# Half as many warming products from the second group on, and PSUM banks dealt anew between three kinds of tile

## The chip, the cores and the metric

The kernel runs on one core of a Trainium2 chip. The metric is device time in microseconds (us), from the start of the execution to its end, as the median of several runs. The core's engines are TensorE (PE, whose weight loads are listed apart as PEld), VectorE (DVE), ScalarE (ACT), GpSimd (POOL) and SyncE (SP), whose queue issues most of the transfers between DRAM and the on-chip memory. TensorE writes its products to PSUM, which has eight banks here: a tile of 128 x 512 numbers of four bytes fills one.

## The reference

Three layers follow each other, with 4 batches, 8 heads, 768 steps and a head size of 48.

```python
# layer 1: a delta-rule scan over t, per batch and head
k_n = k / (norm(k) + 1e-6)
y[t]  = q[t] @ state
state = state + beta[t] * outer(k_n[t], v[t] - k_n[t] @ state)
# layer 2: x = y with heads side by side
u, v = split(gelu(x @ w_in)); v = layernorm(v) * g_ln
x = x + (u * (w_sg @ v + b_sg)) @ w_out
# layer 3: xk, xr mix x with the step before it
out = sigmoid(xr @ w_r) * (relu(xk @ w_k)**2 @ w_v)
```

## The kernel before, in words

The scan is cut into 12 chunks of 64 steps. Two chunks make a *group*, so there are six groups, 0 to 5. The 32 pairs of batch and head are held in two halves, `o` = 0 and 1. A chunk of a half goes through six stages, each a burst of small products and then one step on another engine that the next stage needs:

- `st_rq` (L444, L446): keys times state into tile `rk`, and the query products into tile `qk`. Then DVE forms the residual `r` (L424), ACT copies `qk` out (L453) and POOL masks it (L454).
- `st_d0` (L432): the solver's matrix times `r`. Then ACT copies out `u` (L461).
- `st_l` (L468): a correction into `rk`. Then DVE forms `r` again (L424).
- `st_d1` (L432 again): the second solve. Then ACT copies the result to `SQ` (L479).
- `st_s` (L488): the new state into `sps`. Then ACT copies it out (L494).
- `st_y` (L502): the output `y` into a tile `ms`. Then ACT copies it to `yst` (L507) and SP sends it on as `xT` (L523, L527).

The two halves run three stages apart, so TensorE alternates between them: 24 *points* (places in the program at which one stage of one half stands) make a group. On PE, DVE, ACT and POOL the instructions stay in the order in which this code writes them. SP's order is made by the compiling layer.

At each point other work is put around the stage. `background` gives DVE (with ACT and POOL behind it) a slice of the next group's triangular solver (L321 to L412), of a layer norm (L586 to L602), and of a weight's conversion (`narrow`, L157 to L168). `fill` gives TensorE work of layer 2 for the previous group: `v` products (L567, then Gelu on ACT at L576) and `u` products (L618, Gelu at L622), and every other point of a stretch also the key products of a later group (`gram`, L298 and L300, copied out at L307). Where `fill` has no such work left it calls `keep_warm` (L659), which multiplies a zero tile `warm` by itself: a 128 x 128 weight load and a 128 x 512 product, into a tile `ms` that nobody reads. How many there are comes from the stage's entry in `UNITS`, in units of one such product, with the fraction carried over in `idle`. In a steady group the layer's work runs out for eight points in a row, around the group's start.

PSUM is dealt out so: `sps0` and `sps1` have a bank each, and the pool `ps2` gives two banks to `rk`, two to `qk` and two to `ms`. `ms` is what `bank()` returns, and `gram`, `st_y`, the `v` and `u` products and `keep_warm` all share it in turn. A tile that is asked for waits until the tile which held its bank before has been read out.

After the scan follow layers 2 and 3, in which all eight banks belong to one pool, and which the change doesn't touch.

Of the kernel before, what the change touches and what calls it, by code (L numbers as in the profile page):

```python
# [7 lines left out]
F32 = mybir.dt.float32  # L8
# [12 lines left out]
P = 128  # L21
C = 64
# [6 lines left out]
LJ = 2  # L29
LJ0 = 7  # L30
SV = 60
B0 = 1.4
PRE = 0.8
GRAM0 = 17
# [40 lines left out]
def fused_kernel(  # L75
# [144 lines left out]
    with ExitStack() as at:  # L220
# [3 lines left out]
        ps2 = at.enter_context(tc.tile_pool(name="ps2", bufs=2, space=PSUM))  # L224
# [34 lines left out]
        banks = [ps2]  # L259

        def bank():
            return banks[0].tile([P, 8, C], F32, name="ms")

        Sps = [ps1.tile([P, 8, D], F32, name=f"sps{o}") for o in range(2)]
        warm = ap1.tile([P, P], mybir.dt.bfloat16, name="warm")
# [17 lines left out]
        def gram(g, parts=((0, 64),)):  # L283

            GD = ap1.tile([P, 32, NU], F32, name="GD")
            GL = ap2.tile([P, NU, 32], F32, name="GL", bufs=NGL)
            GLs[g] = GL

            def half(i, c0, c1, j):
                t = kT[2 * g + i // 2]  # L290
                if j == 0:
                    GDs["ps"] = bank()
                gps = GDs["ps"]
                for p in range(4 * j, 4 * j + 4):
                    u = (i % 2) * 8 + p
                    for h in range(2):
                        r = 64 * (1 - h)
                        T.matmul(gps[r:r + 32, p, c0:c1], lhsT=t[r:r + 64, u, 0:32],  # L298
                                 rhs=t[r:r + 64, u, c0:c1], start=True, stop=True)
                        T.matmul(gps[r + 32:r + 64, p, c0:c1], lhsT=t[r:r + 64, u, 32:64],  # L300
                                 rhs=vw2(t, r, 64, u * C + 32, [(0, (c1 - c0) // 32), (1, 32)]),
                                 start=True, stop=True)
                if j:
                    for x, c in ((GD[:, :, 8 * i:8 * i + 8].rearrange("p j u -> p u j"), 0),
                                 (GL[:, 8 * i:8 * i + 8, :], 32)):
                        if c0 <= c < c1:
                            A.activation(x, gps[:, :, c:c + 32], AF.Copy, scale=-1.0)  # L307

            GDs[g] = GD
            return [[(-GU, lambda i=i, j=j, c=c: half(i, *c, j)) for j in range(2)]  # L310
                    for c in parts for i in range(4)]
# [104 lines left out]
        def scale_v(s):  # L416
            G.tensor_tensor(vt[s], vt[s], vw(neTs[s // 2], NPR * (s % 2), [(1, NPR), (0, D)]),
                            op=ALU.mult)
# [3 lines left out]
        def residual(s, o):  # L422
            t = ap2.tile([P, 8, D], F32, name="r32")
            V.tensor_tensor(t, vt[s][:, 8 * o:8 * o + 8, :], RQs[o][:, :, 0:D], op=ALU.add)  # L424
            RQs[o, "r"] = t
# [10 lines left out]
        def st_rq(s, o):  # L436
            cur, k0 = SQ[o][s % 2], 8 * o
            R = RQs[o] = ps2.tile([P, 8, D], F32, name="rk")
            Q = ps2.tile([P, 8, C], F32, name="qk")
            for p in range(8):  # L440
                for h in range(2):
                    r, b0 = 64 * (1 - h), 64 * h
                    k = kT[s][r:r + 64, k0 + p, :]
                    T.matmul(R[r:r + 64, p, :], lhsT=k, rhs=cur[h][r:r + 64, p, 0:D],  # L444
                             start=(p == 0), stop=True, skip_group_check=True)
                    T.matmul(Q[b0:b0 + 64, p, :], lhsT=k, rhs=cur[h][r:r + 64, p, D:],  # L446
                             start=(p == 0), stop=True, skip_group_check=True)
            yield
            residual(s, o)
            for h in range(2):  # L450
                b0 = 64 * h
                pt = cur[h][b0:b0 + 64, :, D:]
                A.activation(pt, Q[b0:b0 + 64], AF.Copy, scale=-1.0)  # L453
                G.affine_select(out=pt, in_=pt, pattern=[[0, 8], [1, C]],  # L454
                                compare_op=ALU.is_gt, fill=0.0, base=0, channel_multiplier=-1)
# [40 lines left out]
        def st_y(s, o):  # L496
            g, cur = s // 2, SQ[o][s % 2]
            yps = bank()
            for p in range(8):
                for h in range(2):  # L500
                    b0 = 64 * h
                    T.matmul(yps[b0:b0 + 64, p, :], lhsT=cur[h][:, p, 0:64],  # L502
                             rhs=cur[h][:, p, D:], start=True, stop=True)
            yield
            if s % 2 == 0:
                ysts[o] = ap2.tile([P, 8, P], F32, name="yst")
            A.activation(ysts[o][:, :, C * (s % 2):C * (s % 2) + C], yps, AF.Copy, scale=-1.0)  # L507
            if s + 2 < 12:
                load_q(s + 2, o)
            if s % 2:  # L510
                store_x(g, o, ysts[o])
                after(LAGX, lambda: x_split(g, o))
            if o == 1:
                if s + 2 < 12:
                    load_tok(s + 2)
                    after(4, lambda: scale_v(s + 2))
                load_k(s + NKT)
# [15 lines left out]
        later, vstat, streams, point = [], {}, [], [0, 0]  # L533

        def after(n, f):
            later.append((point[0] + n, f))
# [95 lines left out]
        def fill(n):  # L632
            n += owed[0]
            while n > 0 and (units or opened[0]):
                if not opened[0]:
                    done = min([i for i, _ in running] + [n_jobs - len(jobs)])
                    ready = [u for u in units if done >= (6, 12)[u[2]]]
                    if ready:
                        units.remove(ready[0])
                        opened[0] = ready[0][1]()  # L640
                    else:
                        break
                w, f = opened[0].pop(0)
                f()
                n -= w
            owed[0] = min(n, 0)
            if n > 0 and point[0] < 144:
                idle[0] += n
                keep_warm(int(idle[0]))
                idle[0] -= int(idle[0])  # L650

        idle = [0]

        def keep_warm(n):

            if n > 0:
                o = bank()[:].rearrange("p a b -> p (a b)")
                for _ in range(n):
                    T.matmul(o, lhsT=warm, rhs=vw(warm, 0, [(0, 4), (1, P)]), start=True, stop=True)  # L659

        def background(t):

            for e in [e for e in later if e[0] <= point[0]]:
                later.remove(e)
                e[1]()
            i = 0
            while t > 0:
                ready = [e for e in streams if e[0] <= point[0]]
                if not ready:
                    return  # L670
                kinds = [[e for e in ready if e[2] == k] for k in ("ln", "solve")]
                kinds.append([e for e in ready if any(e[1] is j for _, j in running[:2])])
                turn = [k[0] for k in [kinds[j] for j in TURN[point[1]]] if k]
                e = turn[i % len(turn)]
                try:
                    c = next(e[1])
                    if isinstance(c, tuple):
                        e[0] = point[0] + c[0]
                        if c[0] == 0:
                            c[1]()  # L680
                        elif c[1] is not None:
                            after(c[0], c[1])
                    else:
                        t -= c
                    i += 1
                    streams.remove(e)
                    streams.append(e)
                except StopIteration:
                    streams.remove(e)
                    running[:] = [r for r in running if r[1] is not e[1]]  # L690
# [31 lines left out]
        def whole(job):  # L722
            for _, f in job:
                f()

        stages = [st_rq, st_d0, st_l, st_d1, st_s, st_y]
        rest = [lambda j=j: whole(j) for j in diag[4:]]
        k = 0
        while any(e[2] == "solve" for e in streams):
# [9 lines left out]
            if 0 in neTs and 1 not in GDs:  # L739
                after(SV, lambda: scale_v(1))  # L740
                body = st_rq(0, 0)
# [14 lines left out]
        def run(fn, s, o):  # L756
# [11 lines left out]
            if point[0]:  # L768
                background(BUDGET[stages.index(fn)] * (B0 if g == 0 else 1))
            while len(jobs) > n_rest and len(running) < RUN[0]:  # L770
# [20 lines left out]
        while opened[0]:  # L791
            fill(1)
# [164 lines left out]
    ms = {}  # L957
# [112 lines left out]
```

## Time and profile before

| | us |
|---|---|
| time, median of 3 runs | 815.54 (814.7 to 817.19) |
| the profiled execution, its own time | 811.44 |
| its span, first to last instruction | 809.7 |
| PE busy in the span | 747.1 (92%) |
| DVE busy | 583.3 (72%) |
| ACT busy | 344.3 (43%) |
| POOL busy | 186.9 (23%) |
| mean granted TensorE clock | 0.970 |

The profile is of one execution, and its time lies 4.1 us under the median of the others. Times within it count from the span's start. The stage loop begins at about 50 us, its group 1 at 103, group 2 at 160.6, group 3 at 213.8, group 4 at 267 and group 5 at 314; the scan's last stage ends near 374. A matmul's end is modelled, and a new one starts before the one ahead has ended, so for PE the distances from start to start tell more than the busy share. A bracket behind a row of the timeline gives the idle time of that engine before it and what ended it.

### The profile page before, as it was taken

How to read it: one execution, taken by the hardware profiler on the slowest of the kernel's cores; microseconds unless marked ns; L12 is line 12 of the kernel's file. 1: busy time of each engine (PE TensorE's matmuls, PEld its weight loads, DVE VectorE, ACT ScalarE, POOL GpSimd, SP SyncE). 2: the span in 40 equal slices, each digit the busy share in tenths (PEclk: the TensorE clock that was granted, in tenths of full speed). 3: DMA queues.
4: the chain of work that ended last, by engine and by line, in shares of the span. 5: the costliest groups of instructions: out<-in, count | busy, mean ns of one | idle time of the engine just before them, and what ended most of it. 6: DMA issues, size and time to landing. Idle time of an engine off the chain costs nothing.

```text
span 809.7 us, 23901 instructions
## 1 busy us (share of the span) xinstructions
PE 747.1 (92%) x10206; PEld 656.5 (81%) x10206; DVE 583.3 (72%) x1253; ACT 344.3 (43%) x681; POOL 186.9 (23%) x197
## 2 busy tenths in 40 slices
PE   3368999999999998978989899899999999999998
PEld 3335667768778676767889799799999999999998
DVE  7989999689699698234779896988945655653442
ACT  2213454465555644634632231316744544542331
POOL 4125342232131323323324453340000000000000
PEclk9978999999999999989999889899999999999999
DMA  8403353354353443437987646449200000000000
GB/s 231 90 27 100 91 118 87 95 155 140 94 150 83 132 121 92 137 99 184 277 266 247 202 128 194 145 127 292 59 30 21 20 20 20 20 21 30 11 20 30
DMA packets 84970, 89.21 MB, mean 110 GB/s; under 512 B 25856, under 2 KB 68992, under 8 KB 84864
## 3 DMA queue, kind: packets, MB, share of 16 engines
q1 hardware_dynamic: 80128, 78.64, 32.8%
q0 software_dynamic: 4736, 9.04, 4.2%
q8 instruction: 80, 1.31, 0.7%
q14 instruction: 26, 0.21, 0.1%
HBM read 56.86 MB, written 26.08 MB: 102 GB/s over the span
## 4 chain that ended last, share of the span: by engine, by line
PE 60%; DVE 18%; DMA 7%; issue 6%; POOL 3%; ACT 2%; SPq 2%; DVEq 0%; POOLq 0%; ACTq 0%
PE ms L139 32%; PE ms L618 5%; PE ms L659 4%; PE rk L432 3%; PE ms L567 3%; PE ms L298 2%; DVE tmp L321 2%; PE ms L884 2%; DMA raw<-in_w_k_dram 2%; PE ms L502 2%; PE rk L468 2%; PE sps L488 2%; PE rk L444 2%; POOL na L168 1%; DVE na L157 1%
## 5 line engine op out<-in xcount | busy, mean ns | idle before, releaser
L168 POOL TENSOR_TENSOR na<-raw,na 128x256 f32<-128x256 f32 (+2 forms) x43 | 40.2, 938 | 149.7 <-DVE raw L167 110.0
L659 PE MATMUL ms<-warm 128*128 128x512 bf16 x222 | 62.1, 405 | 9.0 <-DVE warm L407 9.0
L139 PE MATMUL ms<-wvh,sh 128*128 128x384 f32 x192 | 64.9, 338 | 0.0
L139 PE MATMUL ms<-wvl,sh 128*128 128x384 f32 x192 | 64.9, 338 | 0.0
L139 PE MATMUL ms<-wvh,sl 128*128 128x384 f32 x192 | 64.8, 338 | 0.0
L139 PE MATMUL ms<-xm_hi,wkh 128*128 128x384 f32 x192 | 64.1, 334 | 0.0
L139 PE MATMUL ms<-xm_lo,wkh 128*128 128x384 f32 x192 | 64.1, 334 | 0.0
L139 PE MATMUL ms<-xm_hi,wkl 128*128 128x384 f32 x192 | 64.1, 334 | 0.0
L432 PEld LDWEIGHTS rk<-r,DT 32*32 32x32 f32 x1536 | 36.2, 107 | 28.7 <-DVE r L424 18.5
L111 DVE TENSOR_TENSOR sl<-r,sh 128x384 fp32r<-128x384 f32 x64 | 35.8, 559 | 30.3 <-ACT sh L108 30.3
L454 POOL TENSOR_SCALAR_AFFINE_SELECT SQ<-SQ 64x512 f32<-64x512 f32 x48 | 36.4, 759 | 86.6 <-ACT SQ L453 85.1
L432 PE MATMUL rk<-r,DT 32*32 32x48 f32 x1536 | 42.8, 205 | 13.0 <-DVE r L424 12.7
L424 DVE TENSOR_TENSOR r<-vk,rk 128x384 f32<-128x384 f32 x48 | 26.4, 549 | 38.4 <-PE rk L468 23.9
L108 ACT ACTIVATE sh<-r 128x384 fp32r<-128x384 f32 x64 | 33.6, 525 | 35.9 <-DVE r L990 35.9
L108 ACT ACTIVATE raw<-na 128x256 fp32r<-128x256 f32 (+2 forms) x31 | 13.7, 442 | 80.0 <-POOL na L168 78.1
L1006 DVE TENSOR_TENSOR ob<-th,ms 128x384 f32<-128x384 f32 x24 | 13.3, 553 | 43.3 <-PE ms L139 43.3
L300 PE MATMUL ms<-kT 64*32 64x64 f32 (+1 forms) x896 | 30.6, 225 | 13.9 <-issue 13.9
L618 PE MATMUL ms<-xh,wiu_hi 128*128 128x256 f32 x144 | 43.0, 298 | 0.0
L618 PE MATMUL ms<-xh,wiu_lo 128*128 128x256 f32 x144 | 42.9, 298 | 0.0
L618 PE MATMUL ms<-xl,wiu_hi 128*128 128x256 f32 x144 | 42.3, 294 | 0.6 <-issue 0.6
L990 DVE TENSOR_TENSOR r<-r 128x384 f32<-128x384 f32 x64 | 35.5, 554 | 9.6 <-ACT r L989 9.6
L157 DVE TENSOR_SCALAR na<-raw 128x256 uint32<-128x256 uint32 (+2 forms) x43 | 19.8, 461 | 30.1 <-DMA raw<-in_w_v_dram 7.7
(158 smaller groups left out, 2295.3 us busy)
## 6 DMA issues: line engine op xcount, KB each, us to landing
kT<-in_kt_d_dram SPq DMA_DIRECT2D x12, 512.0 KB, 4.5
u_d<-ug SPq DMA_DIRECT2D x48, 128.0 KB, 2.0
u<-u_d SPq DMA_DIRECT2D x8, 768.0 KB, 5.3
vn_d<-v SPq DMA_DIRECT2D x23, 256.0 KB, 3.9
vst<-vn_d SPq DMA_DIRECT2D x23, 256.0 KB, 3.4
SQ<-in_q_d_dram SPq DMA_DIRECT2D x48, 96.0 KB, 3.6
vk<-in_vk_dram SPq DMA_DIRECT2D x24, 192.0 KB, 3.9
vk<-in_vk_dram SPq DMA_DIRECT2D x12, 384.0 KB, 4.1
```

The source lines that it names most:

```text
L108: A.activation(hi, src, AF.Copy)
L111: eng_lo.tensor_tensor(lo, src, hi.bitcast(F32), op=ALU.subtract)
L139: T.matmul(pt, lhsT=a, rhs=b, start=(i == 0), stop=(i == n - 1))
L157: V.tensor_scalar(a, w_hi, 0x7FFFFFFF, None, op0=ALU.bitwise_and)
L168: G.tensor_tensor(af, f, af, op=ALU.add)
L300: T.matmul(gps[r + 32:r + 64, p, c0:c1], lhsT=t[r:r + 64, u, 32:64], rhs=vw2(t, r, 64, u * C + 32, [(0, (c1 - c0) // 32), (1, 32)]), start ...
L424: V.tensor_tensor(t, vt[s][:, 8 * o:8 * o + 8, :], RQs[o][:, :, 0:D], op=ALU.add)
L432: T.matmul(RQs[o][b0:b0 + 32, p, 0:D], lhsT=DT[b0:b0 + 32, u0 + p, :], rhs=t[b0:b0 + 32, p, :], start=True, stop=True, skip_group_check=True)
L454: G.affine_select(out=pt, in_=pt, pattern=[[0, 8], [1, C]], compare_op=ALU.is_gt, fill=0.0, base=0, channel_multiplier=-1)
L618: T.matmul(vstat["u"][:, 2 * P * d:2 * P * d + 2 * P], lhsT=w[:, c, ds_], rhs=a[:, c].rearrange("p b t -> p (b t)"), start=first, stop=last)
L659: T.matmul(o, lhsT=warm, rhs=vw(warm, 0, [(0, 4), (1, P)]), start=True, stop=True)
L990: V.tensor_tensor(r, r, r, op=ALU.mult)
```

## The change

Two things are changed. From point 24 (the start of group 1) on, an idle unit counts half in `fill`, so that half as many warming products are issued. And the six banks of `ps2` are dealt as two for `rk`, one for `qk` and three for `ms`.

```diff
+WARM = 0.5
...
         def bank():
-            return banks[0].tile([P, 8, C], F32, name="ms")
+            return banks[0].tile([P, 8, C], F32, name="ms", **({"bufs": 3} if banks[0] is ps2 else {}))
...
             R = RQs[o] = ps2.tile([P, 8, D], F32, name="rk")
-            Q = ps2.tile([P, 8, C], F32, name="qk")
+            Q = ps2.tile([P, 8, C], F32, name="qk", bufs=1)
...
             if n > 0 and point[0] < 144:
-                idle[0] += n
+                idle[0] += n if point[0] < 24 else WARM * n
                 keep_warm(int(idle[0]))
                 idle[0] -= int(idle[0])
```

In the built program 222 warming products become 164. They stand in 56 runs before and after: no run vanishes. The runs of groups 1 to 5 are, before and after: 24 to 12 products in group 1, then 28 to 14, 27 to 13 and 27 to 14 around the starts of groups 2, 3 and 4, and 11 to 6 in group 5.

On PE, at the start of group 2, this is a run between two solves (`rk<-r,DT`) of `st_d1` and `st_d0`. Before:

```order
L432 MATMUL rk<-r_2616,DT 32x48 x16
L659 LDWEIGHTS warm
L659 MATMUL ms<-warm 128x512
L659 LDWEIGHTS warm
L659 MATMUL ms<-warm 128x512
L659 LDWEIGHTS warm
L659 MATMUL ms<-warm 128x512
L659 LDWEIGHTS warm
L659 MATMUL ms<-warm 128x512
L432 MATMUL rk<-r_2706,DT 32x48 x16
```

After (every line number is one higher):

```order
L433 MATMUL rk<-r_2604,DT 32x48 x16
L660 LDWEIGHTS warm
L660 MATMUL ms<-warm 128x512
L660 LDWEIGHTS warm
L660 MATMUL ms<-warm 128x512
L433 MATMUL rk<-r_2692,DT 32x48 x16
```

The run goes from four products to two, and nothing else moves.

On PE, in group 1, these are the end of a `v` product, the start of the next, and the `st_y` behind it (`ms<-SQ`), with the semaphores that each waits for. Before:

```order
L567 MATMUL ms<-wiv_hi,xl 128x512
L567 MATMUL ms<-wiv_hi,xh 128x512 [waits PE_49]
L567 MATMUL ms<-wiv_lo,xh 128x512
L567 MATMUL ms<-wiv_hi,xl 128x512
L502 MATMUL ms<-SQ_109 64x64 [waits Activation_49]
```

After:

```order
L568 MATMUL ms<-wiv_hi,xl 128x512
L568 MATMUL ms<-wiv_hi,xh 128x512
L568 MATMUL ms<-wiv_lo,xh 128x512
L568 MATMUL ms<-wiv_hi,xl 128x512
L503 MATMUL ms<-SQ_109 64x64 [waits PE_49]
```

`st_y` waited for ACT, which had to read the `v` product out of the bank that `st_y` gets. With three banks it gets one whose last user was TensorE itself.

On SP the order changes in a few places, all of one kind. This is the queue around `st_y` of half 1 at the start of group 2 (`vk`: values and keys of a coming chunk; `raw`: a weight to be converted; `SQ`: queries). Before:

```order
L148 DMA raw<-in_w_out_dram 128x384
L247 DMA vk<-in_vk_dram 64x768
L607 DMA vn_d<-v 128x512
L247 DMA vk<-in_vk_dram 64x768
L253 DMA SQ_115<-in_q_d_dram 48x8x64
L253 DMA SQ_116<-in_q_d_dram 48x8x64
L523 DMA xT<-yst 48x3x128 x4
L527 DMA xT<-yst 32x2x128
L527 DMA xT<-yst 16x2x128 x2
L527 DMA xT<-yst 32x2x128
L248 DMA vk<-in_vk_dram 128x768
```

After:

```order
L248 DMA vk<-in_vk_dram 64x768
L608 DMA vn_d<-v 128x512
L254 DMA SQ_115<-in_q_d_dram 48x8x64
L254 DMA SQ_116<-in_q_d_dram 48x8x64
L524 DMA xT<-yst 48x3x128 x4
L528 DMA xT<-yst 32x2x128
L528 DMA xT<-yst 16x2x128 x2
L528 DMA xT<-yst 32x2x128
L248 DMA vk<-in_vk_dram 64x768
L249 DMA vk<-in_vk_dram 128x768
```

The second half of the values now stands behind the eight `xT` transfers, and the `raw` load stands some 20 rows further down the queue. DVE, ACT and POOL have the same instructions in the same order as before.

## Rows read from the trace of the kernel before

**Rows 1.** The page: busy time, share of the span and instructions of each engine.

```profile
PE 747.1 (92%) x10206; PEld 656.5 (81%) x10206; DVE 583.3 (72%) x1253; ACT 344.3 (43%) x681; POOL 186.9 (23%) x197
```

**Rows 2.** Busy time by stretch: stretch, its length, busy and count by engine, clock, DMA.

```profile
159.80:173.00 13.20, 13.20 (x289) 7.92 (x289) 7.61 (x24) 8.94 (x16) 3.89 (x5) 1.00 0.53 153
275.40:319.10 43.70, 39.54 (x868) 30.73 (x866) 42.26 (x84) 21.80 (x40) 14.07 (x14) 1.00 0.40 107
```

**Rows 3.** The timeline of PE, start of group 2: start, us, instruction.

```profile
163.66 1.04 PE L659 MATMUL ms<-warm 128*128 128x512 bf16 x4
164.63 0.87 PE L432 MATMUL rk<-r,DT 32*32 32x48 f32 x32
...
166.40 0.92 PE L488 MATMUL sps<-SQ,vk 64*48 64x48 f32 x32
...
168.00 0.87 PE L468 MATMUL rk<-u,GL 32*32 32x48 f32 x32
168.80 0.60 PE L659 MATMUL ms<-warm 128*128 128x512 bf16 x2
169.34 1.15 PE L502 MATMUL ms<-SQ 128*64 128x64 f32 x32
...
177.31 0.87 PE L432 MATMUL rk<-r,DT 32*32 32x48 f32 x32
...
178.91 0.40 PE L567 MATMUL ms<-wiv_hi,xl 128*128 128x512 f32 x1
179.34 1.15 PE L502 MATMUL ms<-SQ 128*64 128x64 f32 x32
```

**Rows 4.** The timeline of ACT in the same stretch.

```profile
163.78 1.00 ACT L479 ACTIVATE SQ<-rk 64x384 f32<-64x384 f32 x2 [0.74 <-PE rk L432]
...
165.54 0.49 ACT L461 ACTIVATE u<-rk 128x384 f32<-128x384 f32 x1
```

**Rows 5.** The timeline of DVE in the same stretch.

```profile
161.84 0.56 DVE L424 TENSOR_TENSOR r<-vk,rk 128x384 f32<-128x384 f32 x1 [3.33 <-PE qk L446]
...
168.99 0.55 DVE L424 TENSOR_TENSOR r<-vk,rk 128x384 f32<-128x384 f32 x1 [2.92 <-PE rk L468]
...
176.71 0.54 DVE L424 TENSOR_TENSOR r<-vk,rk 128x384 f32<-128x384 f32 x1
```

**Rows 6.** The timeline of DVE, its first two residuals after the start of group 1.

```profile
111.73 0.56 DVE L424 TENSOR_TENSOR r<-vk,rk 128x384 f32<-128x384 f32 x1 [1.01 <-PE rk L468]
...
118.74 0.54 DVE L424 TENSOR_TENSOR r<-vk,rk 128x384 f32<-128x384 f32 x1
```

**Rows 7.** The timeline of PE, group 1, where `st_y` follows two `v` products.

```profile
121.48 0.39 PE L567 MATMUL ms<-wiv_hi,xl 128*128 128x512 f32 x1
123.31 1.86 PE L502 MATMUL ms<-SQ 128*64 128x64 f32 x32 [1.43 <-ACT v L576]
...
126.25 1.15 PE L468 MATMUL rk<-u,GL 32*32 32x48 f32 x32
```

**Rows 8.** The timeline of ACT there.

```profile
121.36 1.28 ACT L576 ACT_TABLE_LOAD   x1
```

**Rows 9.** Busy time by stretch (columns as in rows 2), just behind that wait.

```profile
124.00:126.00 2.00, 2.00 (x24) 1.48 (x22) 1.97 (x4) 0.60 (x1) 0.00 (x0) 0.50 0.55 221
```

**Rows 10.** The timeline of PE in group 0, at the low clock.

```profile
75.65 1.49 PE L432 MATMUL rk<-r,DT 32*32 32x48 f32 x32
...
78.89 1.52 PE L488 MATMUL sps<-SQ,vk 64*48 64x48 f32 x32
```

**Rows 11.** The waits of PE from 275 to 323.5 us: us in total, times, longest.

```profile
PE rk L432 <- DVE r L424: 3.5, 3, 2.6
```

**Rows 12.** The timelines of SP and of POOL, start of group 2.

```profile
174.49 3.34 SPq L527 DMA_DIRECT2D xT<-yst  x4
...
176.31 1.53 POOL L417 TENSOR_TENSOR vk<-vk,neT 128x768 f32<-128x768 f32 x1
185.87 1.69 POOL L111 TENSOR_TENSOR xl<-xT,xh 128x768 fp32r<-128x768 f32 x1 [8.03 <-DMA kT<-in_kt_d_dram]
```

## The prediction

> **What bounds the kernel now.** I read the page first: PE is busy for 92% of the span [rows 1]. That alone doesn't say that a product less is time won, because a warming product keeps PE busy while it waits for somebody. So the question is asked stretch by stretch: when PE is through with a warming run, has the input of the next stage long been there?
>
> I then read PE's timeline at the start of group 2. A run of four warming products followed by a stage takes 0.97 us from its start to the stage's (163.66 to 164.63), a run of two 0.54 us (168.80 to 169.34) [rows 3]. So a product costs (0.97 - 0.54) / 2 = 0.215 us. The stages behind the runs start at once, and the rows of ACT and DVE tell how long their inputs had been ready. The solve at 164.63 needs the residual that ended at 161.84 + 0.56 = 162.40: 2.2 us early [rows 3, 5]. `st_s` at 166.40 needs the copy that ended at 164.78: 1.6 us early. `st_l` at 168.00 needs the one that ended at 166.03: 2.0 us early [rows 3, 4]. So in this stretch nobody is waited for but PE itself. The other side says the same: DVE is busy for only 7.61 of 13.2 us there [rows 2], and sits idle for 3.33 and 2.92 us until PE has done the stage that its next residual needs [rows 5]. The same eight points stand around the starts of groups 3 and 4, with the same runs and the same two DVE waits.
>
> It isn't so everywhere. From the residual at 168.99 on DVE doesn't wait again, and the solve at 177.31 starts 0.06 us after its residual ended (176.71 + 0.54) [rows 3, 5]: from 168.99 to 177.31 the chain runs through DVE. In group 4 it stays there much longer: from 275.4 to 319.1 DVE is busy for 42.26 of 43.7 us [rows 2], and PE waits three times for a residual, 3.5 us in all [rows 11]. In group 1 DVE is nearly full too: 1.01 us of idle before the residual at 111.73, none before the one at 118.74 [rows 6].
>
> Last, one wait for a bank is visible. At 123.31 `st_y` starts after 1.43 us of idle, released by a Gelu that had to load its table first (1.28 us at 121.36) [rows 7, 8]. The stretch behind runs at a granted clock of 0.50, which is 1.2 of 2.4 GHz [rows 9].
>
> **The change, part by part.** The profiled execution took 811.44 us, and the sum is made against it. Its time is 4.1 us under the median of 815.54, and I take the same difference off the median.
>
> *Warming products, groups 2 to 4.* A product left out before the `st_l` that DVE waits for moves DVE's next residual up by its 0.215 us. A product left out behind that `st_l` brings PE sooner to the solve at 177.31, where it has to wait for DVE, and gives nothing. Counting the runs of the built program between one such solve and the next `st_l`: in group 2 the runs 3, 5, 4, 4, 3 become 1, 3, 2, 2, 1 (10 out), in group 3 2, 5, 4, 4, 3 become 1, 2, 3, 1, 2 (9 out), in group 4 the same become 2, 2, 2, 2, 1 (9 out). That is 28 x 0.215 = 6.0 us. It stays under DVE's idle time of 3.33 + 2.92 us per group [rows 5], so DVE can follow. The inputs keep their lead: two points lie between a stage and the one that needs it, they shrink by some four products or 0.9 us, and the leads were 1.6 to 2.2 us. The other 13 products of these groups are costed at nothing, because DVE's solver work covers them. If DVE did not, they would give 13 x 0.215 = 2.8 us more.
>
> *Warming products, group 1.* Twelve go, but DVE's only idle time is the 1.01 us at 111.73 [rows 6]. So the gain lies between 0 and 1.0 us, and I take 0.8.
>
> *Warming products, group 5.* The chain comes back to PE at 319. Five products go, three of them ahead of the `st_y` from which the next transfers start: 0.6 us, between 0 and 5 x 0.215 = 1.1.
>
> *A third bank for `ms`.* In the built order the `st_y` of 123.31 no longer waits for ACT. From the start of the last `v` product at 121.48 to this stage are 1.83 us, where a product and a change of stage take about 0.3 (the 0.54 of a run of two, less 0.215) [rows 3, 7]: 1.5 us. If PE doesn't stand idle there, the clock doesn't fall. What that is worth comes from group 0 at the low clock, where a solve, a run of four and the start of `st_s` take 3.24 us (75.65 to 78.89), against 1.77 for the same at 164.63 to 166.40: a factor of 1.83 [rows 3, 10]. The 2.94 us from 123.31 to 126.25 would be 1.6, and the `st_l` behind them 0.87 instead of 1.15 [rows 3, 7]: 1.6 us together. DVE lets PE be earlier there only as far as its own idle time goes, so I take 3.0 us of the 3.1. The bounds are 0 (something else holds `st_y`) and 3.1. In the later groups the same wait is short: in group 2 the `st_y` at 179.34 starts 0.43 us after the product before it, 0.1 more than the 0.3 of a free change of stage [rows 3]. Two `st_y` a group wait for such a bank, in groups 2 to 4: 6 x 0.1 = 0.6 us, between 0 and that.
>
> *One bank for `qk`.* Its reader is ACT's copy (L453), and the next query products come six or seven points later. At 1.77 us a point (164.63 to 166.40 [rows 3]) that is over 10 us for a copy like that at 163.78, of 1.00 us [rows 4]. The five points between hide it: cost nothing. If ACT were that late, TensorE would stop at `st_rq` with all stages behind it, but then it would stop today for other copies first.
>
> *The moved transfers.* The second half of the values goes behind the `xT` transfers, whose last issue ends at 174.49 + 3.34 = 177.83. POOL's scaling of the values, now at 176.31, has to wait until it lands, some us later. Behind it on POOL stands work that starts at 185.87 after 8.03 us of idle [rows 12]: whatever lands up to 185.87 - 1.53 = 184.3 is covered. The scaled values are needed a chunk later. Cost nothing. Without that cover `xl` and the first `v` products would be late by some us once a group. The `raw` loads also slip, but each is used more than a group after its issue.
>
> The sum is 6.0 + 0.8 + 0.6 + 3.0 + 0.6 = 11.0 us: 800.4 for an execution like the profiled one, and **804.5** for the median. Behind the scan I expect the whole shift to be kept, since the tail starts from the last `st_y`.
>
> **Rivals.**
>
> *Clock, slower.* The products are there to keep TensorE occupied, and PE's own waits may grow once they are half gone. If a sparse stretch of eight points fell to the low clock, its 13.2 us would become (13.2 - 14 x 0.215) x 1.83 = 18.6, so 5.4 us worse than now and 7.4 worse than forecast. One stretch makes 812; two make 819, so from two of five on the kernel is slower. All of groups 1 to 4 would give about 834. For it speaks that the clock had fallen by 124, just behind 1.43 us of idle [rows 7, 9]. Against it, PE stays without a gap in these stretches, since it is the one that is waited for; a new wait of 0.6 to 0.9 us arises only at the solves of 177.31 and its likes, and in group 1. The Trainium skill, page "TensorE: Matmul & The Clock Gate", section "Why this matters for your kernels", says to leave no idle gaps between bursts of matmuls in mid-kernel, because the engine then falls back to its low clock. By that rule removing fillers is a danger wherever they hide a wait; the trace agrees as to the fall behind 123.31, and shows no wait under the fillers of groups 2 to 4.
>
> *DVE takes it all.* DVE might have no free time to give, say because its solver work is really paced by ACT or POOL. Then only the banks give something: 3.0 + 0.6 = 3.6 us, 811.9. The two idle times in rows 5 speak against it.
>
> *PE alone is the bound.* Then all 58 products count: 58 x 0.215 = 12.5, with the banks 16.1, and 799.4. Against it stand rows 2 (group 4) and 11.
>
> *The third bank does nothing*, because the wait moves to the next tile on the same Gelu: 3.6 less, 808.1.
>
> **How the numbers follow.** The forecast has a chance of 0.60 (its own range is 801 to 807.5), the idle bank 0.09, PE alone 0.10, DVE taking it 0.09, one stretch at the low clock 0.05, two or more 0.07. The range of **799 to 812** leaves out the last and some of the edges. A change of 0.3% (2.4 us) is about what a measurement here can tell from none. Faster by more than that means under 813.1: all but the two-stretch case and part of the two cases near 812, so 0.85. Same 0.08, slower 0.07.
>
> **What would show it.** Right: the waits of DVE at the starts of groups 2 to 4 shrink from 3.3 and 2.9 us by about 2 us per group, PE waits for a residual by 0.6 to 0.9 us where the solve of 177.31 stands, the 1.43 us on the Gelu are gone, and the clock stays at 1.00 from 100 us to the end of group 4. The scan ends 11 us earlier, and the layers behind it take what they took. Wrong: a clock of 0.50 in a sparse stretch, DVE's waits unchanged, a bank wait that comes back at another `ms` tile, or `xl` late behind the scaling on POOL.

## The result and the profile after

The changed kernel takes 806.96 us (median of 4 runs, 803.99 to 810.94) where the kernel before takes 816.37 in the same series (4 runs, 814.70 to 817.73): a ratio of 0.9894, with a 95% interval of 0.9864 to 0.9924. By the medians that is 9.4 us less, by the ratio 8.7; the forecast was 11.0, or 804.5 us. The number alone settles little: the rival in which the third bank does nothing stood at 808.1, which is nearer to 806.96 than 804.5 is.

The profiled execution of the change took 810.94 us with a span of 809.2, nearly that of the kernel before, at a mean clock of 0.949 instead of 0.970. So it is one of the longer ones, and its span alone shows no gain. The page's row on PE, beside [rows 1]:

```profile
PE 740.4 (91%) x10148; PEld 656.2 (81%) x10148; DVE 580.6 (72%) x1253; ACT 343.5 (42%) x681; POOL 187.1 (23%) x197
```

PE's timeline at the start of group 2, which answers to [rows 3] (start, us, instruction):

```profile
161.98 0.60 PE L660 MATMUL ms<-warm 128*128 128x512 bf16 x2
162.52 0.87 PE L433 MATMUL rk<-r,DT 32*32 32x48 f32 x32
...
163.85 0.92 PE L489 MATMUL sps<-SQ,vk 64*48 64x48 f32 x32
...
165.03 0.87 PE L469 MATMUL rk<-u,GL 32*32 32x48 f32 x32
...
173.49 0.87 PE L433 MATMUL rk<-r,DT 32*32 32x48 f32 x32
```

From the solve to `st_l` are 2.51 us (162.52 to 165.03) where there were 3.37 (164.63 to 168.00): 0.86 us, which is four products at 0.215. No bracket stands behind these rows, so no input was late. The timeline of DVE there, beside [rows 5]:

```profile
160.59 0.55 DVE L425 TENSOR_TENSOR r<-vk,rk 128x384 f32<-128x384 f32 x1 [2.80 <-PE qk L447]
...
166.01 0.56 DVE L425 TENSOR_TENSOR r<-vk,rk 128x384 f32<-128x384 f32 x1 [1.19 <-PE rk L469]
...
172.89 0.55 DVE L425 TENSOR_TENSOR r<-vk,rk 128x384 f32<-128x384 f32 x1
```

DVE's waits went from 3.33 and 2.92 us to 2.80 and 1.19, 2.26 us together, against a forecast of about 2; at the starts of groups 3 and 4 they shrank by 1.98 and 2.21 us. Between the second and the third residual lie 6.88 us where there were 7.72 [rows 5]: DVE's part of the chain became shorter too, which nobody had forecast. The rows that differ in it, before:

```profile
169.91 1.71 DVE L334 TENSOR_TENSOR rn_y<-rn_y,ss 128x32 f32<-128x32 f32 x1
...
174.89 0.68 DVE L321 TENSOR_TENSOR tmp<-NT,Yt 128x64 f32<-128x64 f32 x1
```

And in the change:

```profile
167.85 1.23 DVE L345 TENSOR_TENSOR rn<-rn 128x32 f32<-128x32 f32 x1
...
171.42 0.33 DVE L322 TENSOR_TENSOR tmp<-NT,Yt 128x64 f32<-128x64 f32 x1
```

Each of the two long instructions takes 0.19 us in the other kernel. They began during an operation of GpSimd (`xl`, 169.89 to 171.57 before, 167.34 to 169.02 in the change) and ended just behind it. That is 1.52 us too much before and 1.04 in the change; with the 0.35 us of the other row it makes 0.83 of the 0.84 us.

Busy time by stretch shows what was lost (columns as in rows 2: PE, PEld, DVE, ACT, POOL, granted clock, DMA share, GB/s). The first and the last stretch are at the low clock, the first behind a wait of 1.67 us for the residual (solve at 121.15); the one between is group 4, beside [rows 2], where DVE is still busy for 40.61 of 43.0 us:

```profile
122.10:125.40 3.30, 3.30 (x32) 2.46 (x34) 2.51 (x7) 2.37 (x3) 0.00 (x0) 0.50 0.50 129
...
266.00:309.00 43.00, 39.55 (x897) 31.20 (x896) 40.61 (x82) 23.24 (x42) 13.77 (x14) 1.00 0.45 124
309.80:323.30 13.50, 13.23 (x180) 11.26 (x180) 5.16 (x14) 5.43 (x10) 2.76 (x3) 0.50 0.25 75
```

The last stretch, 13.5 us at a granted clock of 0.50 (1.2 of 2.4 GHz), stands right behind PE's wait for the residual at the start of group 5:

```profile
307.16 0.28 PE L619 MATMUL ms<-xh,wiu_hi 128*128 128x256 f32 x1
310.07 1.49 PE L433 MATMUL rk<-r,DT 32*32 32x48 f32 x32 [2.63 <-DVE r L425]
```

The kernel before has this wait too [rows 11], but in its profiled execution the clock stayed up behind it, and the solve took 0.87 us instead of 1.49:

```profile
319.13 0.87 PE L432 MATMUL rk<-r,DT 32*32 32x48 f32 x32 [2.62 <-DVE r L424]
```

Where time went is best read from leads: the start of one stage in the profiled execution of the kernel before, less the start of the same stage in another kernel's. The columns are named by the start in the kernel before; all but two are `st_y`, 302.33 and 348.53 are solves that wait for a residual. The last is the difference of the spans.

| us ahead of the kernel before | 112.30 | 155.10 | 208.50 | 261.69 | 302.33 | 326.41 | 348.53 | span |
|---|---|---|---|---|---|---|---|---|
| the change, first profile | -0.2 | 0.7 | 3.6 | 6.2 | 9.1 | 5.1 | 3.9 | 0.5 |
| the change, again | 0.6 | 2.9 | 5.5 | 8.1 | 11.1 | 7.7 | 7.8 | 6.9 |
| the kernel before, again | -0.3 | 1.3 | 0.9 | 0.9 | 0.9 | -2.1 | -2.1 | -4.1 |
| only the halving | 0.5 | -3.2 | -0.7 | 1.3 | 4.0 | 4.7 | 4.7 | 3.2 |
| only the banks | -1.5 | 2.7 | 2.7 | 3.1 | 3.3 | -0.1 | 0.2 | -0.4 |
| banks, late products out | -1.5 | 2.6 | -1.3 | -4.6 | -7.4 | -10.1 | -10.8 | -14.3 |
| the change, no product from group 1 on | 0.1 | 2.4 | 5.4 | 6.9 | 10.5 | 7.6 | 5.6 | 4.2 |
| the change, scaling issued later | 0.9 | 3.8 | 6.6 | 9.2 | 11.4 | 8.1 | 7.3 | 4.0 |
| the change, scaling of one chunk out | -0.1 | 3.5 | 6.6 | 9.2 | 12.2 | 9.5 | 8.9 | 5.0 |
| the change, 18 products added | 0.1 | 1.5 | 4.9 | 7.4 | 9.4 | 10.3 | 12.4 | 7.8 |
| the change, 21 products added | 0.2 | 1.3 | 1.3 | 2.7 | 5.7 | 6.5 | 11.5 | 9.2 |
| before, 10 products added | 0.9 | 3.0 | 3.0 | 3.0 | 3.0 | 1.9 | 6.3 | 7.4 |

One row is one execution, and the stretches at 0.50 fall differently in each. How far two executions of one kernel can be apart shows in the third row: 1.3 us ahead and 4.1 behind. The ratios are of all runs, not of these executions. Differences of leads are taken before rounding.

### The profile page after: what moved, and what is told of

Its sections match the earlier page's. It is cut to its first block, busy times and chain, and to the rows that moved or that the text cites. A ratio compares the mean times of both kernels' runs of the same rounds, so it can differ in the third digit from the quotient of the medians.

```text
span 809.2 us, 23785 instructions
## 1 busy us (share of the span) xinstructions
PE 740.4 (91%) x10148; PEld 656.2 (81%) x10148; DVE 580.6 (72%) x1253; ACT 343.5 (42%) x681; POOL 187.1 (23%) x197
## 4 chain that ended last, share of the span: by engine, by line
PE 60%; DVE 17%; DMA 7%; issue 7%; POOL 3%; ACT 2%; SPq 2%; DVEq 0%; POOLq 0%; ACTq 0%
PE ms L140 32%; PE ms L619 5%; PE ms L568 4%; PE rk L433 4%; PE ms L660 3%; PE ms L299 3%; DVE tmp L322 2%; PE ms L885 2%; PE ms L503 2%; PE rk L469 2%; PE sps L489 2%; PE rk L445 1%; POOL na L169 1%; DVE r L425 1%; DVE na L158 1%
## 5 line engine op out<-in xcount | busy, mean ns | idle before, releaser
L433 PEld LDWEIGHTS rk<-r,DT 32*32 32x32 f32 x1536 | 38.0, 110 | 32.8 <-DVE r L425 23.6
L433 PE MATMUL rk<-r,DT 32*32 32x48 f32 x1536 | 44.7, 210 | 17.6 <-DVE r L425 17.3
L660 PE MATMUL ms<-warm 128*128 128x512 bf16 x164 | 50.4, 420 | 9.0 <-DVE warm L408 9.0
L425 DVE TENSOR_TENSOR r<-vk,rk 128x384 f32<-128x384 f32 x48 | 26.3, 547 | 35.8 <-PE rk L469 13.5
L158 DVE TENSOR_SCALAR na<-raw 128x256 uint32<-128x256 uint32 (+2 forms) x43 | 20.1, 467 | 33.8 <-DMA wk_dl<-na 9.3
L299 PEld LDWEIGHTS ms<-kT 64*32 64x32 f32 x896 | 26.0, 120 | 20.4 <-issue 13.2
```

The costliest lines, as they stand in the source:

```text
L433: T.matmul(RQs[o][b0:b0 + 32, p, 0:D], lhsT=DT[b0:b0 + 32, u0 + p, :], rhs=t[b0:b0 + 32, p, :], start=True, stop=True, skip_group_check=True)
```

## The experiments

The code cuts show single lines, as they differ from the change where no other kernel is named; `...` stands for lines left out.

**The change again.** No edit.

> The changed kernel again, unaltered. In its profiled execution (span 809.2 us) the scan was 10.0 us ahead of the kernel before at 292 us and only 4.4 us ahead at 328, with a granted clock of 0.50 from about 310 to 323 us, behind a wait of 2.6 us for a residual that stands in the kernel before too. Theory 'chance of the execution': that low stretch is not in every execution; where it is missing the span is about 5 us shorter, 803 to 804, and the times fall in two heaps. Theory 'caused by the change': the stretch is there in every execution, also in the ones at 804, and the spread comes from somewhere else. Median ratio to the kernel before 0.987 to 0.991 by both.

Median 806.15 us of 6 runs, ratio 0.9902 (0.9869 to 0.9935) to 814.47. The profiled execution took 804.45 us, and it has a stretch at 0.50 from 307.6 to 317.8 too, 10.2 us long; the stretch at 122 is not there. So "caused by the change" would fit the place at 308, were it not for the kernel before. Of the other theory two things failed: the time of 804.45 us has the stretch in it, and the six times form no two heaps.

**The kernel before again.** No edit.

> The kernel before, unaltered, once more with a profile. Its profiled execution took 811.44 us at a mean clock of 0.970, 4.1 us under the median. Theory 'chance of the execution': it holds more time at a clock of 0.50 in another execution, at the same waits (the 2.6 us at 319, the 1.43 us at 123), at a total time nearer to 815. Rival: it has the same stretches, and the difference between the profiled execution and the median is spread over the span.

One execution, 815.5 us at a clock of 0.956. Its stretch behind the 2.62 us wait is there:

```profile
318.27 0.87 PE L432 MATMUL rk<-r,DT 32*32 32x48 f32 x32 [2.62 <-DVE r L424]
...
320.42 1.49 PE L432 MATMUL rk<-r,DT 32*32 32x48 f32 x32
```

The second solve takes 1.49 us instead of 0.87, and between 302.33 and 326.41 this execution loses 2.9 us against the first. And at 123, behind the same 1.43 us on the Gelu, its clock stays up, where the first execution fell. So whether the clock falls behind a given wait differs between executions of one kernel. Of the ten profiles in which the 2.2 to 2.6 us wait at the start of group 5 stands, eight fall in it or within 2 us behind it (not the first of the kernel before, not that of the halving alone). The profile on which the forecast was built is one of the two.

**Only the warming products**, and **only the banks**:

```diff
-name="ms", **({"bufs": 3} if banks[0] is ps2 else {}))
+name="ms")
-            Q = ps2.tile([P, 8, C], F32, name="qk", bufs=1)
+            Q = ps2.tile([P, 8, C], F32, name="qk")
```

> Only the warming products are halved; the banks are dealt as before. The forecast's sum gives 11.0 less 3.6 = 7.4 us under the kernel before, a ratio of 0.991. The rival, from the trace of the changed kernel, where the solve ahead of the freed output stage waited 1.67 us for a residual: the third bank gave nothing, and this kernel is as fast as the whole change, 0.988 to 0.989.

```diff
-                idle[0] += n if point[0] < 24 else WARM * n
+                idle[0] += n
```

> Only the banks are dealt anew; all 222 warming products stand. The forecast's sum gives 3.6 us under the kernel before, a ratio of 0.9955 (812.5 for 816). The rival, that DVE's residual takes the place of the bank's wait in group 1, gives 0 to 0.7 us, 0.999 to 1.000.

The products alone: 809.48 us of 11 runs, 0.9941 (0.9912 to 0.9969), 4.8 us by the ratio. The banks alone: 811.40 us of 12 runs, 0.9966 (0.9941 to 0.9991), 2.8 us. Together 7.6 us, of the 8.0 that the change gives in the same series (0.9902). The forecast had 7.4 and 3.6. The rival that the banks give nothing would have put the products alone at 0.988 to 0.989, outside their interval; the banks' own interval only just leaves out 1.000. In the profile of the products alone the wait for the bank is still there, 1.34 us at 124.25, behind 2.05 us for the residual at 120.83, and the clock is at 0.50 from 122.6 to 132.8.

The two profiles also show which part brought this new wait for a residual in group 1. With the halving alone:

```profile
117.87 1.48 POOL L418 TENSOR_TENSOR vk<-vk,neT 128x768 f32<-128x768 f32 x1
...
118.09 1.34 DVE L322 TENSOR_TENSOR tmp<-NT,Yt 128x64 f32<-128x64 f32 x1
...
120.23 0.55 DVE L425 TENSOR_TENSOR r<-vk,rk 128x384 f32<-128x384 f32 x1
...
120.83 0.87 PE L433 MATMUL rk<-r,DT 32*32 32x48 f32 x32 [2.05 <-DVE r L425]
```

With the banks alone:

```profile
118.87 0.23 DVE L322 TENSOR_TENSOR tmp<-NT,Yt 128x64 f32<-128x64 f32 x1
...
120.24 0.54 DVE L425 TENSOR_TENSOR r<-vk,rk 128x384 f32<-128x384 f32 x1
...
120.63 1.48 POOL L418 TENSOR_TENSOR vk<-vk,neT 128x768 f32<-128x768 f32 x1
```

With the banks alone GpSimd's scaling of the values stands behind the residual, DVE needs 7.01 us from residual to residual (113.23 to 120.24), as in the kernel before [rows 6], and no solve waits there. With the halving alone TensorE's query products are earlier, GpSimd's mask and scaling follow them, and the same stretch takes DVE 8.60 us (111.63 to 120.23). So the wait comes from the halving, not from the third bank.

**No warming product from group 1 on.**

```diff
-WARM = 0.5
+WARM = 0.0
```

> The change with no warming product at all from group 1 on (the factor 0 in place of 0.5). The forecast's way of counting: 27 more products go ahead of the correction stages in groups 2 to 4, 27 x 0.215 = 5.8 us, which DVE's left idle time (2.80 and 1.19 us a group) still covers, so a ratio of about 0.982. The clock rival: with nothing between the stages PE now waits for its inputs, the granted clock falls to 0.50 at the starts of groups 2 to 4, some 5 us each, and the kernel is no faster than the change, or slower: 0.990 to 1.005.

808.81 us of 6 runs, 0.9925 (0.9896 to 0.9955): no gain over the half. Windows of the stretch at the start of group 3:

```profile
209.00:212.50 3.50, 2.93 (x96) 2.47 (x96) 3.19 (x10) 3.33 (x6) 2.12 (x4) 1.00 0.27 57
212.60:222.60 10.00, 10.00 (x189) 8.59 (x191) 8.39 (x34) 6.70 (x11) 3.07 (x3) 0.50 0.55 156
```

The rival named in the prediction, the clock in a sparse stretch, comes true here at 212 us: PE had no wait of more than 0.3 us between 205 and 215. The clock also fell at 110 and 274 us, but there PE had just waited, 1.54 us for ACT and 1.70 us for a residual. From 155.10 to 302.33 the lead grows by 8.2 us, as in the change: what the further products gave went into these falls and into new waits at the solves (1.18, 0.92 and 1.70 us); no run separates the two.

**Warming products where TensorE stands idle** (also the best version).

```diff
+EXTRA = {32: 6, 113: 5, 120: 10}
...
             fill(more + UNITS[stages.index(fn)])
+            keep_warm(EXTRA.get(point[0], 0))
```

> The change, with 21 warming products added only where TensorE of the changed kernel stands idle ahead of a solve that waits for a residual: 6 in group 1 (idle 1.7 to 2.1 us at 121), 5 in group 4 (1.3 to 1.4 us at 291 to 293), 10 at the start of group 5 (2.63 us at 308 to 310). By the price of 0.215 us each they fit into the idle time, so they cost nothing. Theory 'the fall of the clock is due to these waits': the stretch at a clock of 0.50 around 308 to 323 us, which took 4.4 and 5.6 us in the two profiles of the change, is gone, and the kernel is some 3 to 4 us faster than the change: a ratio to the kernel before of 0.985. Rival 'the fall comes anyway' (from the sparse stages as such, or from the waits in the 40 us before): the stretch stays, ratio 0.990, as the change.

800.98 us of 6 runs, 0.9819 (0.9781 to 0.9857) to 815.90: the fastest kernel of this study, 14.9 us under the kernel before. Between 83 and 410 us only one stretch at 0.50 is left, from 198.8 to 202.2. Yet the leads speak against the clock as the whole cause: between 326.41 and 348.53 this kernel gains 5.0 us more, because the wait at 341 us is gone. DVE converts a part of the weight `w_out` there, ahead of a residual, and in the kernel before it waits for the load of that part, which SP had only just issued:

```profile
344.02 0.91 SPq L148 DMA_DIRECT2D raw<-in_w_out_dram  x2
...
346.47 0.26 DVE L157 TENSOR_SCALAR na<-raw 128x192 uint32<-128x192 uint32 x1 [7.20 <-DMA raw<-in_w_out_dram]
```

In the change's second profile the load was issued at 336.28, likewise behind the `xT` transfers. Here it had moved ahead of them:

```profile
317.31 0.40 SPq L150 DMA_DIRECT2D raw<-in_w_out_dram  x1
```

DVE's conversion then starts at 332.09 without a wait, and the residual behind it ends in time.

**The same with 7 instead of 10 products at point 120**, which leaves the load behind `xT`.

Against the kernel just above:

```diff
-EXTRA = {32: 6, 113: 5, 120: 10}
+EXTRA = {32: 6, 113: 5, 120: 7}
```

> As the kernel with 21 added products, but 7 instead of 10 at the start of group 5 (18 in all). By that the raw load of w_out in SP's queue stays where the change has it, behind the eight transfers of xT; with 10 it stood ahead of them, and TensorE's wait of 4.85 us at 341 for a residual behind that load was gone. Theory 'two causes': of the 14.9 us that the kernel with 21 products was faster than the kernel before, some 5 came from the moved load and not from the clock; here the wait of 4.5 to 5.5 us near 340 is back, and the ratio is 0.986 to 0.989. Rival 'the clock alone': the clock stays up as there, and the ratio is again 0.982.

805.55 us of 6 runs, 0.9888 (0.9854 to 0.9922) to 814.14, so "two causes" holds by its ratio; the wait came back smaller than I wrote, 2.78 us for 4.5 to 5.5, with the load at 330.79:

```profile
333.31 0.26 DVE L159 TENSOR_SCALAR na<-raw 128x192 uint32<-128x192 uint32 x1 [4.89 <-DMA raw<-in_w_out_dram]
```

At the start of group 5, where 1.11 us of waiting are left, the clock stays up here too; at the 2.78 us wait it is at 0.50, from 335.5 to 342.3. The 18 products are thus worth nothing clear of the noise against the change (0.9888 to 0.9894 or 0.9902), and the moved load, with three products more, 0.7% (0.9819 to 0.9888); 2.9 us of that show in the leads, which grow by 5.0 there and by 2.1 here between 326.41 and 348.53.

**The kernel before with 10 products there.** Against the kernel before:

```diff
             fill(more + UNITS[stages.index(fn)])
+            keep_warm(10 if point[0] == 120 else 0)
```

> The kernel before, all warming products and banks as there, with 10 products more at the start of group 5, where TensorE waits 2.62 us for a residual. They fit into that wait. In SP's queue the raw load of w_out moves ahead of the xT transfers too. Theory: both gains are there without the change, the low stretch behind the wait (in one of two profiles of the kernel before, 6.8 us long) and the wait of 4.3 us at 349: 4 to 6 us, a ratio of 0.993 to 0.995. The change's own part, measured on top of it by the kernel with 21 products, is then 0.982 / 0.994 = 0.988, about what it is without them. Rival: the added products only repair what the change broke, ratio 1.000 here.

806.49 us of 6 runs, 0.9899 (0.9876 to 0.9922). More than expected: one line that adds ten products to the kernel before is worth as much as the whole change; of its gain 4.4 us show between 326.41 and 348.53 (lead 1.9 to 6.3). In its profile the clock is at 1.00 from 62.6 to 380.0 us, and the load has moved ahead of the `xT` transfers (328.46):

```profile
320.64 0.38 SPq L148 DMA_DIRECT2D raw<-in_w_out_dram  x1
```

On top of it the change with 21 products is worth 0.9819 / 0.9899 = 0.992.

**GpSimd's scaling two points later**, and **one scaling left out**:

```diff
-                    after(4, lambda: scale_v(s + 2))
+                    after(6 if point[0] < 48 else 4, lambda: scale_v(s + 2))
```

> The change, with GpSimd's scaling of the values issued two points later in groups 0 and 1. In the change the scaling stands at 117.80 to 119.28 us in one profile, and a solver product of DVE that takes 0.23 us otherwise lasts from 118.02 to 119.35, ahead of the residual for which TensorE waits 2.05 us; in the kernel before the scaling stands at 119.13 to 120.61, behind that residual. Theory 'GpSimd holds DVE up': with the scaling out of the way the residual ends about 1.3 us earlier, the wait of TensorE at 121 falls from 1.7 to 2.1 us to under 0.9 us, and the scan is about 1.3 us ahead of the change from there on; the median falls by as much, to a ratio of 0.988. Rival 'DVE's own work is too long there': the wait stays at 1.7 to 2.1 us, ratio 0.990.

808.06 us of 4 runs, 0.9905 (0.9872 to 0.9938), the wait 2.06 us at 120.42. The edit moved nothing in time: GpSimd had no other work there, and the scaling stood at 117.47, right behind the mask, as ever. So it tells nothing, and I took the scaling away instead:

```diff
-                    after(4, lambda: scale_v(s + 2))
+                    after(4, lambda: scale_v(s + 2) if s != 1 else None)
```

> The change without GpSimd's scaling of the values of one chunk, the fourth, which stands at 117.80 to 119.28 us in one profile of the change; the output is then not the reference's. Issuing that scaling two points later left it at the same time, since GpSimd had nothing else to do, so it is taken away here. Theory 'GpSimd holds DVE up': DVE's solver product at 118.02, 1.33 us long there, takes about 0.23, the residual behind it ends 1.1 to 1.4 us earlier, and TensorE's wait ahead of the solve at 121 falls from 2.05 to under 1.0 us. Rival 'DVE has too much work there': the wait stays at 1.7 to 2.1 us.

The timelines of DVE and POOL in the change, first profile:

```profile
118.08 0.49 DVE L322 TENSOR_TENSOR tmp<-NT,Yt 128x64 f32<-128x64 f32 x1
118.61 0.22 DVE L361 TENSOR_REDUCE Yt<-tmp 128x16 f32<-128x64 f32 x1
118.74 1.43 DVE L158 TENSOR_SCALAR na<-raw 128x192 uint32<-128x192 uint32 x1
```

```profile
117.12 1.37 POOL L455 TENSOR_SCALAR_AFFINE_SELECT SQ<-SQ 64x512 f32<-64x512 f32 x2 [1.74 <-ACT SQ L454]
118.58 1.48 POOL L418 TENSOR_TENSOR vk<-vk,neT 128x768 f32<-128x768 f32 x1
```

Without the scaling, in a kernel that leaves the values of the fourth chunk as they were loaded, DVE and PE:

```profile
118.69 0.23 DVE L322 TENSOR_TENSOR tmp<-NT,Yt 128x64 f32<-128x64 f32 x1
...
119.09 0.25 DVE L158 TENSOR_SCALAR na<-raw 128x192 uint32<-128x192 uint32 x1
```

```profile
120.32 0.87 PE L433 MATMUL rk<-r,DT 32*32 32x48 f32 x32 [0.94 <-DVE r L425]
```

The instruction that began while the scaling ran and ended just behind it (118.74 to 120.17, the scaling to 120.06) takes 0.25 us instead of 1.43. The wait falls from 2.05 (or 1.67) to 0.94 us, as the theory had it, and the lead over group 1 grows from -0.1 to 3.5 us instead of 0.6 to 2.9. The one execution took 806.38 us, so the gain doesn't show in the whole time: the lead of 8.9 us at 348.53 is 5.0 at the end. The Trainium skill, page "SBUF — State Buffer", section "SBUF: two separate sides", states such a lock: GpSimd shares a port pair with VectorE's operations that have two inputs in SBUF or run in a mode with two ports, and whoever starts first holds it for the whole instruction. The rows agree as to the waiting, 1.43 against 0.25 us; the held instruction has one tensor as input, and no run here shows in which mode it ran.

**Only the products that the forecast priced at nothing.** All banks of the change and all products, but none behind the correction stages in groups 2 to 4.

```diff
-                idle[0] += n if point[0] < 24 else WARM * n
+                idle[0] += 0 if 48 <= point[0] < 119 and 4 <= point[0] % 24 < 23 else n
```

> The banks of the change, all warming products of the kernel before, but none in groups 2 to 4 behind the correction stage (points 52 to 54 of group 2 and their likes): 27 products less, and all of them are of those that the forecast costs at nothing. The forecast: these products are covered by DVE's solver, so the kernel is as fast as with the banks alone, a ratio of 0.9966, and TensorE waits some 1.5 us longer at the first solve behind them (177.31 in the kernel before) in each of groups 2 to 4. Rival, TensorE alone is the bound: 27 x 0.215 = 5.8 us less, a ratio of 0.9895.

826.04 us of 4 runs, 1.0128 (1.0087 to 1.0168): both theories fall. Taking these products out doesn't give 0 or 5.8 us, it costs some 13 against the banks alone (0.9966). The wait at the solve of group 3 is 3.77 us, and DVE shows why:

```profile
227.31 1.53 DVE L356 TENSOR_TENSOR NT<-NT,c 128x64 f32<-128x64 f32 x4
228.87 1.47 DVE L321 TENSOR_TENSOR tmp<-NT,Yt 128x4 f32<-128x4 f32 x1
```

The second takes 0.17 us elsewhere. GpSimd's mask runs from 227.38 to 228.77 and its scaling from 228.85 to 230.32. TensorE's query products come 1.69 us after the residual at 223.34, with the banks alone 3.95 us after theirs, so they are two microseconds early; ACT and then GpSimd follow them, and both operations land ahead of the residual for which TensorE waits. From residual to residual DVE needs 9.13 us (223.34 to 232.47), with the banks alone 7.72 (219.40 to 227.12). In the long wait the clock falls (231.6 to 238.4). DVE's lateness is 1.4 us in each of groups 3 and 4 and 0.1 in group 2, while the lead falls by 10.0 us from 155.10 to 302.33; three stretches at 0.50, 17.1 us in all, stand in there. How much of the loss is the clock's, no run separates.

## Why the prediction was right, and where it was not

*Products ahead of `st_l`, groups 2 to 4: 6.0 us, and 0.6 for short waits on banks.* From 155.10 to 302.33 the lead grows by 8.4 us in the first profile and by 8.1 in the second, against 6.6; with the halving alone by 7.2, with the banks alone by 0.6. The mechanism is the forecast one: DVE's waits at the three starts shrink by 6.45 us in the first profile. The rest comes out of the part that I had left to DVE. Between the second and the third residual of groups 2, 3 and 4 lie 6.88, 7.49 and 6.88 us in the change, the same within 0.01 with the halving alone, and 7.72 or 7.73 before and with the banks alone. So this too comes from the halving. That GpSimd's operations, which follow TensorE, lie elsewhere against the same work of DVE is shown by rows in group 2; no run isolates it in these groups. For the same reason the wait of 0.6 to 0.9 us that I foresaw at the solve of 177.31 stands in group 3 alone (0.94 us at 224.66).

*The other 13 products at nothing.* In the change they gave at most the 1.9 us by which DVE's three stretches became shorter, but the reason was too simple: with all 27 of that place gone the kernel is slower by 1.6% than with the banks alone (1.0128 / 0.9966). DVE's time is no fixed cover, since it depends on when GpSimd works beside it.

*Warming products, group 1: 0.8 us, between 0 and 1.0.* This is the term whose mechanism was wrong, and for the same reason: its lower bound of nothing took DVE's time as fixed. The halving moved GpSimd's scaling ahead of the residual, and the solve at 121 now waits 1.67 to 2.06 us in all four profiles of the halved products that have this scaling and no product added. In two of the four the clock fell there (122.0 and 122.6 us). `st_s` also waits 0.79 us for ACT's copy (at 108.7 in the second profile). With the halving alone the lead over group 1 falls from 0.5 to -3.2 us, and the halving as a whole gives 4.8 us by its ratio (2.5 to 7.2) where the forecast had 7.4. In the change the lead over group 1, the bank included, grows by 0.9, 2.3 and 2.9 us (the last with the scaling issued later), where the forecast had 3.8.

*A third bank: 3.0 us.* With the banks alone the wait for the Gelu and the fall of the clock behind it are gone, and the lead at 155.10 is 2.7 us. But 1.6 of the 3.0 us were that low clock, which the kernel before itself doesn't have in every execution (lead 1.3 us at 155.10 when it ran again). By its ratio the new deal of the banks gives 2.8 us (0.7 to 4.8) of the 3.6, with the 0.6 of groups 2 to 4 in both figures.

*Warming products, group 5: 0.6 us.* The fall of the clock at this place hides what they gave; it stays open.

*One bank for `qk`, the moved transfers: nothing.* Right for `qk` and for the values: in group 2 the scaling stands at 179.57, ahead of the limit of 184.3, and `xl` at 181.93, no later than before [rows 12]. That each `raw` load is used more than a group after its issue is not so at the end of the scan: the load issued at 344.02 is used at 346.47 in the kernel before, and DVE waits 7.20 us for it. There the order of SP's queue counts, as the kernels with 10 added products show.

*The clock stays at 1.00 from 100 us to the end of group 4.* True in the second profile and missed in the first (122.0 to 125.4). At the start of group 5, where I foresaw nothing, it fell in both, for 13.6 and 10.2 us, and took 4.0 and 3.3 us of the lead between 302.33 and 326.41. The rival "clock, slower" put this danger into the sparse stretches. With half the products no profile of the change falls at the starts of groups 2 to 4; with none at all one does, at 212 us. The danger came true at a wait that no warming product had ever covered, and that the kernel before pays for too, in one of its two profiles.

*The tail keeps the whole shift.* Between 326.41 and 348.53 the first profile loses 1.2 us, the second nothing; the wait for the `w_out` load is 5.20 and 4.85 us, before 4.30. The last `st_y` of the scan is 4.3 and 8.9 us ahead, not 11. From 348.53 to the end the change loses another 3.4 and 0.8 us; the kernel before, run again, loses 2.0 us there too.

So the forecast was right in its main term, the products ahead of `st_l`, and near in its number partly by luck: groups 2 to 4 gave more than forecast, group 1 less, and the clock at the start of group 5 took some of it in both profiles. What remains open: why the clock falls in some executions and not in others at the same wait, and how much of the last 1 to 2 us is the tail's.

## What to carry to other kernels

A filler is worth taking out where the input of the next stage has long been there: take the ends of the inputs, not the busy share, to tell such a place. Where the engine waits anyway a filler costs nothing and can keep the clock up (three of three profiles at the start of group 5), but 18 such products alone gave no gain clear of the noise here. Before pricing work on a second engine as cover, look at which engine holds it up and who triggers that one: here an earlier TensorE made DVE later, through GpSimd. And a queue whose order is made by the compiling layer can shift with a few instructions elsewhere, so compare its order on every build before a gain is put down to the edit.

## What the runs showed of the hardware

- The same wait of 2.2 to 2.6 us was followed by a clock of 0.50 in 8 of 10 profiles; with 7 or 10 products in it, in none of 3.
- With no warming products the clock fell at 212.5 us though PE had not waited over 0.3 us for anything since 205.
- Instructions of DVE that take 0.17 to 0.25 us lasted 1.23 to 1.71 us when they began during a GpSimd operation on two tensors of 128 x 768 numbers, up to its end; one with a single tensor as input (L158, 1.43 us) did too. A reduction (L361, 0.22 us at 118.61) and a residual, which has one input in PSUM ([rows 5], 0.54 us at 176.71, beside the scaling of [rows 12]), began during such an operation and took their usual time.
